# 44 products of ones with ones on TensorE in front of its first turn of q

## The chip, the cores and the metric

One core of one Trainium2 chip. The metric is the device time of one execution in microseconds. It is read from several runs, and one further execution was taken with a profiler. The engines are TensorE (PE; its weight loads are PEld), VectorE (DVE), ScalarE (ACT), GpSimd (POOL) and SyncE (SP), which issues the transfers.

## The reference

Attention with rotary positions for 4 batches of 8 heads, 576 positions and 64 columns a head, followed by a two-layer network on the 2304 rows of 512 columns:

```
q_rot, k_rot = rotate(q), rotate(k)        # x1*cos - x2*sin, x1*sin + x2*cos
scores = q_rot @ k_rot.T / sqrt(64)
attn = exp(scores - max) / (sum + 1e-9)
x = (attn @ v) as [2304, 512]
h = x @ w_in                               # 512 x 2048
out = (h * sigmoid(h)) @ w_out             # 2048 x 512
```

## The kernel before

Heads are worked in pairs p = 0 to 3 of a batch, positions in blocks of 128. Batch 0 is special. Its q and k are rotated in fp32 and turned (transposed) on TensorE, while those of the later batches are split into two f16 parts and turned by transfers. The products of the network run on TensorE in f16 with each operand split into two parts. Once the first weights are ready, they are woven between the scores of the later batches.

The work is a list of named steps in a `Plan`. A table of numbers and letters, `ORDER`, written out by hand, says in which order they are issued and on which engine (t TensorE, d VectorE, a ScalarE, p GpSimd, s SyncE's queue). Each engine runs its own instructions strictly in that order. A step waits for the steps whose results it reads and for a buffer that it reuses.

At the start, for pair 0, k and q are loaded, and VectorE multiplies each by the sine table into a buffer `rt` (L515, and L517 for the last block) and by the cosine table into a buffer `n`. TensorE then turns both into one place and adds them there (`qP`, L529 to L539): 12 products with the identity matrix, which lie in PSUM afterwards and are copied out to `Tq` and `Tk` (`qE`, L551 on ScalarE, L340 on VectorE). The tag `rt` has two buffers and the tag `n` two. The turn of q writes a tile of the pool `s3`, the turn of k one of the pool `s`. For pair 1, VectorE rotates q and GpSimd rotates k, by the same lines.

Beside this the weights of the network come in blocks of 256 hidden columns. For each block, ScalarE and GpSimd bring the 64-bit numbers into fp32 (L839, L844, L846), VectorE joins their parts (L852, called the weight step below), TensorE sums their squares (`trace`, L365, called the trace products), VectorE and TensorE work out a scale from that, and the weights are split. The scores of batch 0 are L1000, their row maxima L1005, the exponentials L1008, and the turned exponentials L1013.

The order on TensorE at the start is: turn of q for pair 0, turn of k for pair 0, trace products of the first block of w_out, the first pair of scores.

The kernel also holds 84 steps `wk` ("keep"), each of two products of a tile of ones. All of them stand in `ORDER` with the letter z, and a step with z issues nothing. The ones are set by one memset (L1391), number 0 of the plan, which VectorE runs after the rotations of pair 0. They are also read by other products (L591, L701, L769, L895).

Of the kernel before, what the change touches and what calls it, by code (L numbers as in the profile page):

```python
# [21 lines left out]
N_KEEP = 84  # L22
# [22 lines left out]
572a 125d 580s 582a 573d 134s 135t 136d 115p 581a 766t 583d 767d 754t 755a 116t 768a 140s 145s 127t 128a 117d 150s
576s 131d 151t 118s 152d 769t 584s 130p 575d 146d 132t 142d 578a 771t 141p 770a 91s 119t 120d 577a 147p 772d 161s 585a
586p 756t 773a 757d 163s 156t 157d 158d 758a 774t 759t 775a 587d 159p 590a 105d 579d 591d 143t 133a 107d 588a 589d
592t 760a 121a 137d 139d 593d 153d 602s 594p 595d 776t 598p 144a 777d 596p 162s 778a 781t 782d 1963d 740p 786t 787d
783a 597d 123d 779t 780a 600p 788a 1970d 604a 784t 785a 148t 789t 172d 149d 164a 796t 165a 599p 797d 791t 790a 173d
801t 650s 652a 178p 792d 166t 802d 651a 167d 798a 799t 174p 622s 603a 606s 1964t 601p 179d 1966t 803a 623a 608p 605d  # L50
168d 626s 793a 653d 794t 1965d 1967d 800d 624a 180p 625d 804t 811t 812d 795a 806t 1973t 805a 607a 609d 807d 627a 813a
814t 630t 169p 628a 629d 631d 155d 815a 646s 648p 647a 808a 1977d 170d 632a 612t 633d 642s 610t 611d 809t 634t 613d
810a 635d 614t 636p 649d 615d 616d 160d 816t 817d 821t 826t 644a 643a 818a 822d 823a 819t 820a 637p 827d 828a 617p
645d 620p 621d 654a 1978t 618p 824t 1979a 655d 122s 656t 829t 657d 658t 659d 660d 830a 1971t 831t 847t 1968p 1969p
154s 619d 1972a 1974d 661p 1980t 832d 664p 665d 825a 666a 667p 833a 834a 638a 106s 640a 848d 194s 839t 1984d 1985t
1986a 171d 835d 1987t 1981d 692s 639d 1982d 840d 1983p 741p 836d 181a 1975d 837d 1988d 668s 841a 842d 849a 1976d 693a
182d 850d 843d 851d 1989a 1990p 175a 844a 863t 864d 838s 855t 183s 852a 865a 845d 176p 2075t 866a 856d 857a 871t 209p
641d 2076a 2077d 669a 670a 196a 872d 867d 2082t 853d 177s 858d 873a 672s 887t 868d 854s 2078d 671d 662a 2079d 869d
846s 195a 663d 676a 197t 185s 2083a 2084d 888d 673a 674a 2080t 210p 870s 874a 2085a 675d 203p 889a 2091t 678a 677d
859d 890d 211d 860a 198d 199p 200a 2086d 679d 688s 680t 681d 891d 892a 682p 683a 204d 875d 684a 861d 862s 879t 212p  # L60
880d 881a 893d 903t 2092a 685d 2081t 694a 2093d 876a 205d 696s 877d 695d 698p 686a 882a 883d 206a 184s 895t 884p 207d
896d 690a 2098t 2087t 213d 894s 689a 2089t 691d 897a 898a 899d 904d 697a 1991t 2094a 900p 201d 699d 702t 905a 208s
2095d 885d 703d 700a 701d 687d 704t 705d 906d 2090a 186a 919t 706p 2099a 225s 227a 707p 2100d 920d 710a 921a 907d 712a
901p 1992d 1993d 214s 878s 226a 2088a 711d 2101p 911t 908a 912d 913a 886s 718s 902s 2105t 922d 923d 2102d 228t 708a
229d 2106a 927t 943t 714s 720a 909d 713d 234p 928d 2107d 240d 910s 914a 709d 929a 2096t 930a 924a 2097t 722s 230p 241d
925d 935t 187t 719a 715a 235p 2114t 231a 931d 926s 932a 138s 716a 944d 945a 946a 2108a 936d 721d 188d 933d 947d 937a
236d 934s 242p 717d 959t 237a 960d 2103t 724d 938a 189p 939d 948a 726t 723a 949d 950s 940a 725d 941d 2104t 961a 728a
1994t 915d 727d 729d 730t 243p 244d 942s 731d 2109d 962a 916a 917d 951t 190a 952d 191a 732p 918s 983t 963d 984d 1995a
953a 1996d 733p 734a 735d 2110t 985a 238p 193d 192d 2111d 975t 216s 256s 954a 955d 742p 964a 2115a 232d 967t 976d
# [127 lines left out]
def rope_attention_silu_ffn(  # L197
# [61 lines left out]
    live = {}  # L259

    def buf(tag, *key):
        if (tag, key) not in live:
# [8 lines left out]
            if tag == "s3":  # L271
                live["wk"] = live[tag, key]
# [1197 lines left out]
```

## Time and profile before

| what | value |
|---|---|
| median of 3 runs | 623.91 us |
| the three runs | 620.99, 623.91, 627.9 us |
| the profiled execution, its own time | 619.83 us |
| its span, first to last instruction | 618.0 us |
| TensorE busy in the span | 589.6 us (95%) |
| VectorE, ScalarE, GpSimd busy | 473.0, 404.7, 293.7 us |
| mean granted TensorE clock | 0.988 |

The profiled execution is below all three of the other runs. Sums of instructions are made against its 619.83 us; between the span and this time lie 1.8 us. In the views, us are counted from the first instruction. A row of a timeline gives start, length, engine, line, operation, output and inputs, and in brackets the idle time before it with what ended it. The granted clock (PEclk) is 1.00 for 2.4 GHz and 0.50 for 1.2 GHz.

### The profile page before, as it was taken

Reading aid. Unit: us, or ns where it says so; the run is one execution under the profiler, and the core shown is the slowest. Engines: PE = TensorE matmul, PEld = TensorE weight load, DVE = VectorE, ACT = ScalarE, POOL = GpSimd, SP = SyncE. Lnnn points to the kernel's source line nnn. Section 1 sums busy time; section 2 is a strip of 40 time slices with the busy share of each in tenths; the row PEclk is TensorE's granted clock in tenths of the full one; section 3 lists DMA queues with packets and bytes.
Section 4 is the critical chain, followed back from the end, with each engine's and each line's share of the span. In section 5 each row is a group of like instructions: output and inputs, shape, how many; then the busy total and the mean of one; then the engine's idle time right before and its main releaser. Section 6 shows DMA issues by size and latency. Waiting matters only on the chain.

```text
span 618.0 us, 12474 instructions
## 1 busy us (share of the span) xinstructions
PE 589.6 (95%) x4484; PEld 391.1 (63%) x4484; DVE 473.0 (77%) x1046; ACT 404.7 (65%) x846; POOL 293.7 (48%) x306
## 2 busy tenths in 40 slices
PE   1999998999999999999999999999999999999997
PEld 1766755555666666666666666666666666666663
DVE  2788889999898899999888898897888674322312
ACT  3477989998888777777757786677664653322321
POOL 0647665375744676443755356452556662010131
PEclk9977999999999999999999999999999999999999
DMA  7968149997979999998956899887966656100201
GB/s 227 301 223 295 34 111 213 246 224 158 158 154 207 148 166 171 169 192 176 187 101 152 152 201 169 191 147 131 156 110 112 116 101 95 34 2 2 52 1 34
DMA packets 208910, 89.92 MB, mean 146 GB/s; under 512 B 187984, under 2 KB 192592, under 8 KB 208848
## 3 DMA queue, kind: packets, MB, share of 16 engines
q1 hardware_dynamic: 208688, 88.84, 68.8%
q8 instruction: 35, 0.57, 0.4%
q10 hardware_dynamic: 160, 0.30, 0.3%
q14 instruction: 27, 0.22, 0.1%
HBM read 35.49 MB, written 4.72 MB: 65 GB/s over the span
## 4 chain that ended last, share of the span: by engine, by line
PE 74%; DVE 8%; ACT 7%; DMA 5%; issue 3%; SPq 1%; POOL 1%; ACTq 0%; POOLq 0%; DVEq 0%
PE m L1342 27%; PE m L1285 26%; PE s L1128 7%; PE pv L1230 7%; DMA pt<-pn 2%; PE s L1000 2%; ACT e L1162 1%; PE s L1134 1%; DMA w_in<-in_k_dram 1%; DMA vh<-vh 1%; DMA w_out<-in_q_dram 1%; ACT pn L346 1%; DVE small L1149 1%; DVE pn L352 1%; PE s L1013 1%
## 5 line engine op out<-in xcount | busy, mean ns | idle before, releaser
L1285 PEld LDWEIGHTS <-w_in 128*128 128x128 f16 x1728 | 166.6, 98 | 33.0 <-issue 5.0
L1285 PE MATMUL m<-xh,w_in 128*128 128x256 f16 x1024 | 178.2, 273 | 1.8 <-DVE g L1301 1.8
L1342 PE MATMUL m<-w_out,gh 128*128 128x512 f16 x576 | 171.6, 379 | 0.0
L1285 PE MATMUL m<-xl,w_in 128*128 128x256 f16 x512 | 139.5, 273 | 0.0
L1162 ACT ACTIVATE e<-s,small 128x576 f32<-128x576 f32 x128 | 98.8, 772 | 41.4 <-DVE s L1144 19.7
L1342 PE MATMUL m<-w_out,gl 128*128 128x512 f16 x288 | 109.1, 379 | 0.0
L1301 DVE SCALAR_TENSOR_TENSOR g<-g,m 128x512 f32<-128x512 f32 x72 | 49.1, 682 | 60.5 <-ACT g L1297 31.8
L352 DVE SCALAR_TENSOR_TENSOR pn<-e,small,pn 128x576 f16<-128x576 f32 x93 | 83.3, 899 | 6.9 <-ACT pn L346 4.1
L1342 PEld LDWEIGHTS <-gh 128*128 128x128 f16 x576 | 52.0, 99 | 54.5 <-issue 3.1
L1297 ACT ACTIVATE g<-m,small 128x512 f32<-128x512 f32 x64 | 43.7, 683 | 54.9 <-PE m L1285 49.8
L346 ACT ACTIVATE pn<-e,small 128x576 f16<-128x576 f32 x75 | 57.4, 770 | 16.8 <-DVE small L1176 12.9
L1128 PE MATMUL s<-Tk,Tq 128*128 128x512 f16 (+1 forms) x384 | 61.3, 286 | 0.9 <-ACT e L1162 0.6
L1230 PE MATMUL pv<-pt,vh 128*64 128x320 f16 (+1 forms) x504 | 54.1, 290 | 0.0
L340 POOL TENSOR_SCALAR pn<-e,small 128x576 f16<-128x576 f32 x31 | 26.8, 866 | 57.1 <-DVE small L1176 39.2
L1144 DVE TENSOR_SCALAR_CACHE_REDUCE s<-s,small 128x576 f32<-128x576 f32 x59 | 47.9, 817 | 7.2 <-PE s L1128 4.9
L352 DVE SCALAR_TENSOR_TENSOR gl<-g,small,gh 128x512 f16<-128x512 f32 x53 | 43.8, 827 | 11.9 <-ACT gh L346 7.4
L1342 PEld LDWEIGHTS <-gl 128*128 128x128 f16 x288 | 28.2, 98 | 34.0
L355 POOL TENSOR_TENSOR pn<-e,pn 128x576 f16<-128x576 f32 x35 | 45.6, 1302 | 2.9
L1128 PEld LDWEIGHTS <-Tq 128*128 128x128 f16 x384 | 28.9, 99 | 27.2 <-issue 4.5
L1151 DVE TENSOR_REDUCE small<-s 128x1 f32<-128x576 f32 x49 | 36.8, 751 | 9.1 <-PE s L1128 9.0
L340 POOL TENSOR_SCALAR g<-g,small 128x512 f32<-128x512 f32 x19 | 16.4, 863 | 56.1 <-ACT gh L346 37.6
L340 POOL TENSOR_SCALAR e<-e,small 128x576 f32<-128x576 f32 x35 | 28.6, 817 | 29.2 <-ACT pn L346 23.1
(213 smaller groups left out, 1034.0 us busy)
## 6 DMA issues: line engine op xcount, KB each, us to landing
w_in<-in_moe_w_in_dram SPq DMA_DIRECT2D x4, 1024.0 KB, 6.9
w_out<-in_moe_w_out_dram SPq DMA_DIRECT2D x4, 1024.0 KB, 8.9
out_dram<-ob SPq DMA_DIRECT2D x28, 128.0 KB, 2.4
io<-in_q_dram SPq DMA_DIRECT2D x12, 288.0 KB, 3.2
io<-in_k_dram SPq DMA_DIRECT2D x12, 288.0 KB, 3.6
io<-in_v_dram SPq DMA_DIRECT2D x12, 288.0 KB, 4.0
Tk<-Tk SPq DMA_DIRECT2D x22, 144.0 KB, 3.0
ring<-in_moe_w_in_dram SPq DMA_DIRECT2D x3, 1024.0 KB, 7.9
```

The costliest lines, as they stand in the source:

```text
L340: e.tensor_scalar(out=out, in0=in0, scalar1=s1, scalar2=s2, op0=ALU.mult, op1=ALU.bypass if s2 is None else ALU.mult)
L346: act.activation(hi, src, AF.Copy, scale=s)
L352: dve.scalar_tensor_tensor(out=lo, in0=src, scalar=s, in1=hi, op0=ALU.mult, op1=ALU.subtract)
L355: e.tensor_tensor(out=lo, in0=src, in1=hi, op=ALU.subtract)
L1128: pe.matmul(o, tq[:, j, 2 * c:2 * c + 2, :], kt[:, r0:r1, js], start=(n == 0), stop=(n == 1))
L1144: dve.tensor_scalar(out=t, in0=t, scalar1=cc[1], scalar2=None, op0=ALU.mult, op1=ALU.min, accum_out=m_of(1, 2),)
L1162: act.activation(buf("e", i), buf("s", i)[:, 0:S], AF.Exp, bias=m_of(1, 2), scale=-1.0 if fused[i] else cc[0], accum_out=m_of(2, 3),)
L1230: pe.matmul(o[64 * j:64 * j + 64, 0:m], vt[part][:, j, s, :], pt[:, a, j, 0:m], start=(z == 0), stop=(z == len(steps) - 1),)
L1285: pe.matmul(t[:, c, 0:n], w[:, wz, kk, fs], xx[:, kk, 0:n], start=(kk == 0 and x == 0), stop=(kk == KD - 1 and x == 2),)
L1297: act.activation(g[:, :, 0:n], t[:, :, 0:n], AF.Tanh, scale=th_v[units[u][0]][:, i:i + 1])
L1301: dve.scalar_tensor_tensor(out=g, in0=g, scalar=1.0, in1=t, op0=ALU.add, op1=ALU.mult)
L1342: pe.matmul(o, gs[gz][:, c, ts], w[:, wz, c], start=(first and c == 0 and x == 0), stop=(last and c == 1 and x == 2),)
```

## The change

The 84 steps that issue nothing are taken out of the plan, and with them their numbers in `ORDER` (all later numbers become 83 smaller). In their place comes one step `keep` on TensorE: 44 products of the ones (as bf16, 128 by 128) with the ones read four times over (512 columns), each written over the one before in a tile of the pool `s3` that nothing reads. The step stands in `ORDER` second, right behind the memset of the ones, which comes first. The turn of q for pair 0 depends on it. Apart from the two entries and the renumbering the table is the same.

```
-N_KEEP = 84
+N_KEEP = 44
...
-556s 92s 89s 97s 88s 85s 93d 98d 558a 557a 87s 559d 86s 99d 100t 564a 565d 560s 561a 562p 94d 95t 108s 113s 102s 90s
-101a 0d 1z 2z 3z 4z 5z 6z 7z 8z 9z 10z 11z 12z 13z 14z 15z 16z 17z 18z 19z 20z 21z 22z 23z 24z 25z 26z 27z 28z 29z 30z
...
+0d 1t 473s 9s 6s 14s 5s 2s 10d 15d 475a 474a 4s 476d 3s 16d 17t 481a 482d 477s 478a 479p 11d 12t 25s 30s 19s 7s 18a
...
-            if tag == "s3":
-                live["wk"] = live[tag, key]
...
-            n = add("qP", key + (nm,), "t", tr, [n, y, ("ident",)], [nb, rt, sb], it)
+            n = add("qP", key + (nm,), "t", tr, [n, y, ("ident",)] + ([] if p else [("keep",)]), [nb, rt, sb], it)
...
-        w_1 += [("sc2", "w", 1)] + keep if (u, i) == (0, 0) else []
+        w_1 += [("sc2", "w", 1)] if (u, i) == (0, 0) else []
...
-    def add_keep(z):
-        def f(e):
-            if e == "t":
-                if "wk" not in live:
-                    buf("s3", "wk")
-                o = live["wk"][:, 640:1024].rearrange("p (a n) -> p a n", a=3)
-                for _ in range(2):
-                    pe.matmul(o, ones_b, ones_b[:, None, :].to_broadcast([128, 3, 128]), start=True, stop=True)
-
-        return add("wk", (z,), "zt", f, [("ones",)])
-
-    keep = [add_keep(z) for z in range(N_KEEP)]
+    def keep():
+        o = buf("s3", "keep")[:, 0:512].rearrange("p (a n) -> p a n", a=4)
+        for _ in range(N_KEEP):
+            pe.matmul(o, ones_b, ones_b[:, None, :].to_broadcast([128, 4, 128]), start=True, stop=True)
+
+    pl.add(("keep",), "t", keep, [("ones",)], [bk("s3", "keep")])
```

TensorE at the start of the program, before: the branch into the program, then the turn of q for pair 0. `s3` is the tile it writes, `id_t` the identity, `n` and `rt` the two rotated halves.

```order
L1466 UNCONDITIONAL_BRANCH [waits barrier_Pool_Activation_PE_DVE_SP_release]
L529 MATMUL s3_166<-id_t_125,n_162 128x128 [waits DMAHW2_49,DVE_49]
L529 MATMUL s3_166<-id_t_125,rt_151 128x128
...
L534 MATMUL s3_166<-id_t_125,n_162 128x64 [waits DVE_49]
L534 MATMUL s3_166<-id_t_125,rt_151 128x64
...
L529 MATMUL s_187<-id_t_125,n_183 128x128 [waits DVE_49]
```

And now:

```order
L1454 UNCONDITIONAL_BRANCH [waits barrier_Pool_Activation_PE_DVE_SP_release]
L1391 LDWEIGHTS ones_126 [waits DVE_49]
L1391 MATMUL s3_137<-ones_126 128x512
...
L523 MATMUL s3_212<-id_t_125,n_208 128x128 [waits DMAHW2_49,DVE_49,PE_49]
L523 MATMUL s3_212<-id_t_125,rt_197 128x128
...
L528 MATMUL s3_212<-id_t_125,n_208 128x64 [waits DVE_49]
```

In front of the turn stand 44 pairs of a weight load and a product, of which one is shown; the first waits for VectorE's memset, and the turn of q stands behind the last of them.

VectorE around the memset, before: the end of the rotations of pair 0 (`n_183` is k's), the memset, the rotation of q for pair 1 and the weight step of w_out.

```order
L515 TENSOR_TENSOR n_183<-w_in_119,cos_t_123 128x4x64 x2
L517 TENSOR_TENSOR n_183<-ob_138,cos_t_123 128x64
L1391 MEMSET ones_126 128x128
L515 TENSOR_TENSOR rt_210<-w_out_120,sin_t_124 128x4x64 [waits DMAHW0_49,DVE_49,PE_49]
L515 TENSOR_TENSOR rt_210<-w_out_120,sin_t_124 128x4x64
L517 TENSOR_TENSOR rt_210<-ob_138,sin_t_124 128x64
L852 SCALAR_TENSOR_TENSOR w_out_120<-w_out_120 128x1024 [waits DMAHW6_49,Activation_49,Pool_49]
```

The start of VectorE's queue now:

```order
L1454 UNCONDITIONAL_BRANCH [waits barrier_Pool_Activation_PE_DVE_SP_release]
L1385 MEMSET ones_126 128x128
L509 TENSOR_TENSOR rt_193<-w_in_119,sin_t_124 128x4x64 [waits DMAHW7_49,DMAHW1_49]
L509 TENSOR_TENSOR rt_193<-w_in_119,sin_t_124 128x4x64
L511 TENSOR_TENSOR rt_193<-ob_184,sin_t_124 128x64 [waits DMAHW2_49,DMAHW3_49,DMAHW1_49,DMAHW0_49]
```

The memset moved from behind the rotations of pair 0 to VectorE's first place. The other engines' rows are the same. Lines behind the table have numbers smaller by 6 in the changed kernel (L509 is L515 of before).

## Rows read from the trace of the kernel before

**Rows 1.** Page, part 4: the chain that ended last, by engine

```profile
PE 74%; DVE 8%; ACT 7%; DMA 5%; issue 3%; SPq 1%; POOL 1%; ACTq 0%; POOLq 0%; DVEq 0%
```

**Rows 2.** The chain in order of time: start us, length us, what

```profile
0.72 0.47 SPq L818
...
11.26 5.60 DMA w_out<-in_q_dram
...
20.18 1.41 PE s L1000 x7
...
44.61 4.94 PE s L1000 x12
...
606.93 6.49 PE m L1342 x30
```

**Rows 3.** Timeline of TensorE, 0 to 60 us

```profile
13.30 0.48 PE L529 MATMUL s<-id_t,n 128*128 128x128 f32 x1 [13.30 <-DVE n L515]
...
18.50 0.42 PE L539 MATMUL s<-id_t,rt 128*64 128x128 f32 x1
19.07 1.11 PE L365 MATMUL mx<-w_out 128*128 128x128 bf16 x8 [0.15 <-DVE w_out L852]
...
22.48 0.27 PE L529 MATMUL s<-id_t,rt 128*128 128x128 f32 x1
...
28.34 0.27 PE L529 MATMUL s<-id_t,n 128*128 128x128 f32 x1
...
29.81 0.39 PE L365 MATMUL pv<-Tk 128*128 128x128 bf16 x4
...
40.45 0.42 PE L529 MATMUL s<-id_t,rt 128*128 128x128 f32 x1
```

**Rows 4.** Busy time by stretch: stretch, length, each engine's busy us (instructions), PEclk, DMA, GB/s

```profile
13.30:19.00 5.70, 5.62 (x24) 4.23 (x24) 3.05 (x9) 2.25 (x5) 1.12 (x1) 1.00 1.12 322
...
40.00:53.50 13.50, 13.44 (x51) 10.06 (x50) 10.14 (x21) 9.36 (x21) 7.15 (x12) 0.50 0.94 360
...
613.40:615.00 1.60, 0.01 (x1) 0.00 (x0) 0.00 (x0) 0.69 (x1) 0.00 (x0) 1.00 0.53 124
...
616.80:618.00 1.20, 0.00 (x0) 0.00 (x0) 0.00 (x0) 0.00 (x0) 0.00 (x0) 0.50 0.00 0
```

**Rows 5.** Timeline of VectorE, 0 to 70 us

```profile
9.74 0.76 DVE L515 TENSOR_TENSOR rt<-w_in,sin_t 128x256 f32<-128x256 f32 x2 [9.74 <-DMA sin_t<-in_sin_dram]
...
14.17 0.17 DVE L1391 MEMSET ones<- 128x128 f32 x1
16.98 0.76 DVE L515 TENSOR_TENSOR rt<-w_out,sin_t 128x256 f32<-128x256 f32 x2 [2.65 <-DMA w_out<-in_q_dram]
...
17.80 1.22 DVE L852 SCALAR_TENSOR_TENSOR w_out<-w_out 128x1024 int32<-128x1024 int32 x1
...
25.62 1.40 DVE L515 TENSOR_TENSOR rt<-w_in,sin_t 128x256 f32<-128x256 f32 x2
...
28.62 1.24 DVE L852 SCALAR_TENSOR_TENSOR ring<-ring 128x512 int32<-128x512 int32 x1
...
38.65 0.69 DVE L852 SCALAR_TENSOR_TENSOR w_in<-w_in 128x512 int32<-128x512 int32 x1
```

**Rows 6.** Timeline of ScalarE, 0 to 30 us

```profile
16.42 0.63 ACT L551 ACTIVATE Tq<-s 128x576 f32<-128x576 f32 x1
```

**Rows 7.** Timeline of GpSimd, 14 to 31 us

```profile
15.43 1.12 POOL L846 TENSOR_SCALAR w_out<-w_out 128x1024 int32<-128x1024 uint16 x1 [15.01 <-DMA w_out<-in_moe_w_out_dram]
19.01 1.43 POOL L515 TENSOR_TENSOR rt<-w_out,sin_t 128x256 f32<-128x256 f32 x2 [2.45 <-DVE w_out L852]
...
25.14 1.61 POOL L515 TENSOR_TENSOR n<-w_out,cos_t 128x256 f32<-128x256 f32 x2
...
28.58 1.86 POOL L515 TENSOR_TENSOR rt<-w_in,sin_t 128x256 f32<-128x256 f32 x2 [1.37 <-PE s L539]
```

**Rows 8.** What TensorE waited for, 20 to 618 us: us in total, times, longest

```profile
PE m L1285 <- DVE g L1301: 1.8, 2, 1.6
```

More of the change, by code (lines that the diff above doesn't have):

```diff
@@ L45 @@
[L45 to L69, printed above, removed]
@@ new lines @@
+2042p 939d 926t 927d 2043t 891s 899s 137p 921d 940d 2046a 2047d 928d 953t 2044t 138a 139a 954d 2048a 140d 182p 156s
+941a 914a 942d 162s 922d 943s 955a 2049d 929a 1917t 1918a 141d 915d 164s 188p 1919d 930d 923a 944t 956a 945D 2056t
+931d 924d 175a 971t 174a 946d 176t 916s 957a 183d 2050t 184p 2057a 972d 177d 958d 925s 947a 2058d 2059a 932d 933d 178p
+179d 962t 163s 2053t 963D 948d 2054d 2060d 2051d 189p 934s 185a 186p 165a 964d 180d 2063t 965a 966a 190d 166t 187s
+2064a 2061t 167d 2065d 168p 191a 967d 2062t 2070t 968a 150d 169d 192d 2066d 973a 969d 195s 2067d 989t 2068t 170a 171d
@@ new lines @@
+974a 2069t 975d 959a 970s 172d 2071a 990D 211s 949d 950a 960d 951d 961s 991a 952s 2072d 992a 2073d 196a 1007t 993d
+1008d 193s 976d 1009d 980t 981d 2074p 977a 978d 194s 1010a 226p 2077t 197t 2078a 998t 198d 982a 204t 994d 979s 2075t
+205d 206t 995a 2079d 2080p 999d 207d 208p 983a 199d 1000a 220d 1052t 1920t 984a 985d 1011a 986a 996d 200a 1001a 209p
+1002a 213a 987d 210d 181d 1053D 988s 2076t 212a 1034t 1003d 1921a 1054a 1035d 2084t 1922d 1012d 221p 2081d 2082t 1004a
+1005d 997s 214t 662d 201a 202d 1055a 1006s 1013d 203d 1025t 215d 1014d 216p 222p 1036a 2085a 1015s 1026D 1037a 2086d
@@ new lines @@
+1038a 1027d 1028a 1039d 1040p 2083t 217d 223a 1043t 1044d 1923t 1029d 1030d 2087a 1031a 1041d 242s 1032d 1016t 1045a
+1042s 1033s 1046a 1047a 2091t 1017d 1018d 1019a 1924d 2088p 1056d 1057d 1925d 1058a 1020a 2092a 1061t 1062D 1063d
+1021d 1022a 1059d 224p 1048d 1070t 1071d 1023d 1064a 1926t 1060s 2093d 2094a 2089t 1079t 1080d 2090t 2098t 1072a 2052s
+1073a 1049p 1050d 1051s 1088t 227p 228d 218d 1081a 1082a 1083a 1084d 1074d 1024s 2095p 1124t 663d 257d 1085a 225s
+1086d 1087s 1125D 229a 230p 1927a 1928d 231s 1126d 2096t 1127a 1065d 1066d 1075d 1076a 2099a 2097t 1089d 1077d 243a
@@ new lines @@
+2100d 1067p 1068d 1128d 1129d 1090a 1069s 1091a 1092a 1106t 1929t 1107D 1108d 2101p 2102d 2105t 1930a 1931d 1133t
+1130p 1109a 2106a 1110d 1078s 1093d 244a 1131p 2107d 1094a 2108p 1132s 2103t 251d 1134D 258p 1111d 219d 273s 245t
+1097t 246d 1135d 1098D 247p 1136a 2104t 1095d 1137d 2109d 248d 1112a 1096s 1113d 2116t 1151t 252d 259d 1114s 2110t
+2113t 1099a 1100a 232s 1101a 1102d 2117a 253d 260p 1103a 2111a 1138d 261p 2118d 1152D 1153a 1154a 1115t 2114a 2123t
+1104d 1116d 1155a 1117a 1139a 2119d 1105s 1142t 262s 1118a 1140p 2120d 1932t 2124a 254a 1119d 1120d 1178t 1141s 2125d
@@ new lines @@
+2121t 1143d 1144d 1121a 1933d 1156d 1122d 1145a 1169t 1146d 1147d 1179D 2122t 2126a 275a 255d 2127d 282p 1180d 2130t
+1123s 1181a 1157a 1182d 1183d 1170d 1171a 288p 256s 1934d 1160t 2131a 2132d 2133a 2128t 1184p 1185p 1148a 233s 2137t
+274a 1161D 2134d 1162d 1149d 1158d 276t 289d 2129t 1163a 277d 2138a 1164a 283d 1172a 278d 1205t 234a 2139d 2140a 1187t
+284p 1206d 1186s 279d 285a 2135t 1173d 263s 1174d 235t 1188D 1207a 1189d 1175d 1176d 2144t 1190a 290p 291a 286d 236d
+292d 237p 238d 1150s 1159s 1208a 1209a 2141d 1177s 264s 1214t 1191a 1192d 1193d 1223t 1210d 249d 250d 1194d 1211a
@@ new lines @@
+1271a 1257d 1259t 315p 1247a 321d 309p 2161a 1298a 2162d 1286t 1258s 1272a 310a 2055s 322a 1248d 1260d 316a 281d 1261d
+1262a 1941t 323d 317d 326s 1263d 1264d 311d 1299d 1300d 1301p 1232t 1942a 1943d 2163t 2164t 2166a 2167d 2168p 1302d
+296a 1287d 1288a 1249s 1303s 2176t 2169d 1233D 1234d 1235a 297t 1265p 1266d 2170t 2173t 324s 2177a 1273d 1274p 1275p
+327a 298d 1277t 328t 299d 300d 301d 2171a 2178d 302d 1289a 303d 1236d 2179a 318s 1237d 2183t 1238p 1267s 1239p 329d
+2180d 1278D 2181t 1322t 1279d 1290a 2184a 335t 2185d 1280a 2174a 1323d 1331t 1324d 1325a 342s 1332d 336d 2190t 1281d
@@ new lines @@
+1282d 330d 1283a 1291d 1284d 337t 351d 2186p 1276s 2187p 1333d 1240s 2191a 338d 325s 2182t 2188t 331p 332p 343a 344a
+345t 1292p 2192d 1285s 1334a 1326a 1327d 1328a 1335d 1313t 1304t 1293p 1305D 1294s 1314D 1315d 346d 347d 1306d 2193a
+2194d 1329d 2197t 1307a 1944t 1336d 1316a 1337p 349d 350d 339p 1330s 1338p 1339s 2198a 352p 334d 1308a 312d 1340t
+1367t 1368D 1369d 348p 2189t 340d 2195t 341d 1945d 2199d 1946d 1370a 1371a 333d 1317a 1372d 1309d 1318d 1319a 1358t
+1359d 1320d 1360d 1361a 2200p 2201d 1310a 357d 1311d 2204t 1341D 1373a 1342a 1343a 1344a 1947t 1403t 1948d 1404D 1949d
@@ new lines @@
+1362a 1363d 1345d 1321s 1374p 2205a 1405a 1346a 1312s 2196t 1375s 2206d 353p 1347d 373s 1348s 2207a 2208d 2202t 2203t
+1406a 1407a 358d 1408d 1409p 1349t 1350D 1351a 1364a 1410d 1365d 354a 355d 2211t 2212a 1352a 1950t 2213d 2214a 2112s
+1411s 1376t 1353d 1354d 1951a 1377d 1378a 388d 1385t 1379a 2215p 2218t 2209t 1386d 1387d 1366s 2219a 2220d 1388a 1394t
+1395D 1355p 1380a 1381d 1389d 1356p 1357s 1390d 1391d 1392d 2210t 1412t 1382a 1393s 2216t 1413D 1396a 1397a 1414d
+1415a 1416a 359d 1439t 356s 360a 382p 1383d 1384s 1440D 2217t 1441d 1417d 1952d 1398d 2221a 1442a 1418a 1419p 1443a
@@ new lines @@
+387s 380d 1456s 2247d 1464d 1465s 365a 1484t 1485D 1486a 2250t 366t 1472a 367d 1496a 363s 2251a 2252d 1487a 368d 406a
+1488a 1473p 2242t 2253d 2254p 1497d 369a 419d 413d 370a 1498d 1475t 1499a 1476D 1500d 2248t 2257t 2258a 1489d 1502t
+2259d 414p 1503d 2249t 1477a 1474s 372d 1490a 1959t 1478a 1479d 2260a 1504d 1505a 1506a 2261d 1520t 1521d 1960a 393s
+371d 1961d 2264t 1491p 381d 1511t 1501s 1522a 1523a 1507d 1508d 2255t 1509d 1512D 1529t 1530D 1513a 2256t 405a 1524a
+1525d 2265a 2266d 407t 408d 409d 1514a 1515a 1531a 1547t 2267a 1480d 1516d 2268d 1526d 1492s 395s 1510s 1527d 2235s
@@ new lines @@
+1517a 415d 2271t 420p 421p 394s 2272a 1548D 1532a 2262t 2263t 2232s 1538t 410p 416p 396a 422a 2273d 2274p 1518d 1539d
+1528s 397t 1481a 1482d 1519s 1540a 1541a 1542a 417d 2278t 1543d 1483s 1556t 2275d 1549a 1550a 2279a 1557d 418s 1551d
+1544p 1545d 1546s 1558d 2269t 411d 423p 398d 399p 2270t 412d 2280d 1559a 1574t 1552d 1553a 1575d 1576a 2276t 1533d
+2281p 1554d 1577a 1583t 1584d 1585d 1534d 1535p 1536d 2282d 435s 1962t 1578a 1579d 1580a 1565t 2285t 1581p 1555s 1586a
+1537s 2277t 400a 444d 1566d 401a 2283t 1567a 1963d 1964d 1560a 1561d 2286a 1568a 450d 1965t 1569a 2287d 1587d 1619t
@@ new lines @@
+462p 1973d 2332a 1672s 2329t 2330t 1695d 1696d 1697d 1698p 1727t 1728D 1729d 463a 1730a 1974t 2333d 1686a 1687d 1688p
+1709t 1710D 1731a 1711a 1718t 1719d 1732d 1720a 1721a 2338t 1699s 1689d 1736t 2334p 1712a 2335d 1733d 1734d 1735s
+1713a 1714d 465d 1690s 2336t 2339a 1715p 1716p 2340d 2341d 1722a 1737D 1975d 1738a 1739a 1740a 2337t 1772t 1773d 1774a
+1775a 2345t 1717s 1723d 464d 2342d 1724p 1725p 1700t 1754t 1741d 1976d 1701D 1742a 1743d 1744s 1702a 1703a 1755d 2346a
+2343t 1704d 1705d 1756d 1757a 1977t 1978d 2344t 1781t 2115s 2347d 1979d 2356t 1745t 1726s 2348d 1782d 1758a 2349p
@@ new lines @@
+1706d 1707d 2357a 2350t 1783d 1759d 1760d 1784a 1785d 2351a 1708s 2358d 1776a 1786d 1746D 1763t 1764d 2353t 1761p
+1747a 2363t 1762s 1748a 2359p 1787d 1788d 2360p 1790t 1791d 2364a 2365d 1792a 1749a 1777d 1750d 2354a 1980t 2370t
+2366a 1981d 1765a 1751p 1752d 1766a 1789s 1778a 1808t 1753s 2367p 2361t 2362t 1767a 1768d 1982d 2371a 1793a 2372d
+1809D 1779p 1780s 1799t 2377t 1810d 1769d 2355s 1770d 1794d 1771s 1800d 1801a 1811a 1795d 1796a 1797d 1798s 1812a
+1813d 1835t 2368t 2369t 2373p 1802a 2374p 1836D 2378a 1803d 1804d 1814a 1815p 1805d 1816s 1826t 1827D 1828d 1837a
@@ new lines @@
+1838a 1853t 2375t 1983t 1829a 1854D 2379d 1806p 1830d 1831d 2380a 1832d 1833p 1984a 1871t 1855a 1856a 2384t 1872D
+1873a 2381d 1857a 1807s 1874a 1858d 1834s 1859d 2385a 1860p 1875d 1876d 1861s 1877a 1817t 1878p 2376t 1879s 1844t
+1818d 1819d 1820a 1821a 2386d 1845d 2387p 2382t 2383t 1846a 1822d 1839a 1823d 1824d 1840d 1862t 1863D 1825s 1864a
+2388d 1841a 2391t 1865a 1866d 1842d 2392a 1843s 1847a 1848d 2393d 2394a 1849d 1985d 2352s 2395d 1867d 2389t 1850a
+1868p 2390t 1869d 2398t 1851p 2399a 2396t 2400d 2397t 2401p 2402d 1986t 2405t 1870s 1987d 1988d 2406a 1852s 2407d
@@ new lines @@
+1989t 1990a 1991d 2403t 2408a 2409d 2416t 2417a 2404t 2410t 2411a 2412s 2418d 2419a 2420d 2423t 2424a 2425d 2413t
+2426p 2414a 2427d 2421t 2430t 2422t 2428t 2431a 2432d 2433a 2437t 2434d 2438a 2439d 2429t 2435t 2444t 2440a 2415s
+2436t 2441p 2445a 2442t 2446d 2451t 2443t 2447a 2448d 2449t 2452a 2453d 2458t 2450t 2454d 2455d 2459a 2460d 2456t
+2461p 2462d 2465t 2466a 2467d 2457t 2463t 2468a 2476t 2469d 2477a 2464t 2478d 2470t 2479a 2480d 2483t 2471d 2473t
+2481t 2484a 2472s 2485d 2486a 2487p 2474d 2490t 2482t 2488t 2491a 2492d 2493d 2497t 2494d 2292s 2489t 2498a 2475s
@@ L166 @@
+2499d 2500p 2501p 2495t 2504t 2505a 2506d 2496t 2502t 2511t 2507a 2508p 2512a 2503t 2509t 2513d 2514p 2518t 2515d
+2519a 2520d 2510t 2516t 2525t 2521d 2522p 2517t 2523t 2526a 2527d 2524t 2528a 2529d 2530t 2533t 2531d 2534a 2532s
+2535s
 """
```

147 lines of the change are left out of this document (48 added, 99 removed).

## Prediction

> **What bounds the kernel now.** I read the chain that ended last first. TensorE holds 74% of it, and most of the rest is work that hands TensorE its operands [rows 1]. So a microsecond lost or won on TensorE early can reach the end, unless another engine has slack for it. The change touches only the start, so I went on to that stretch of the same chain. There TensorE is not the bound: the chain runs through the transfer of q for pair 1 (issued at 11.26, 5.60 us), VectorE's rotation and weight step on those data, then TensorE's trace products and the first pair of scores, which end at 21.59 [rows 2].
>
> Then TensorE's timeline [rows 3]. Its first turn of q starts at 13.30, and the turns of q and k end at 18.50 + 0.42 = 18.92. One product of a turn takes 0.42 us here, 0.27 us at 22.48, and 0.42 us again at 40.45. The stretches show 0.50 for 40.0 to 53.5, the lower level (1.2 GHz), and 1.00 for 13.3 to 19.0 [rows 4]. I believe the durations, not the 1.00: products as long as those at 40.45 ran at the lower level, and the column shows no change before its first recorded one. So TensorE starts at 1.2 GHz and is at 2.4 GHz by 22.48. That is what warm-up products can change: what stands between 13.30 and about 20 us.
>
> **The change, step by step.** (a) The memset of the ones goes from 14.17 on VectorE to its first place. It takes 0.17 us, and VectorE waits until 9.74 for its first data [rows 5]; at its old place 2.65 us of waiting for a transfer follow it. Cost and gain: nothing. The 84 old entries issued nothing in the kernel before, and their removal costs nothing either.
>
> (b) The 44 products. They can start when the memset is done; the first work of the program, SyncE's first transfer, starts at 0.72 [rows 2], so I put their start at 1.0 (an estimate). Thirty products with 512 columns took 6.49 us at the upper level [rows 2], 0.216 each. All at the upper level: 9.5 us, done at 10.5. All at the lower, at twice the time: 19.0 us, done at 20.0. Before, TensorE went from 0.42 to 0.27 us a product somewhere between 18.92 and 22.48, so after some 6 to 9 us of products. With 6 us at the lower level, 14 products are done by 7.0, and 30 more take 6.5: done at 13.5. That is the start of the turn of q within 0.2 us. ScalarE copies that turn out only at 16.42, behind another instruction [rows 6], so this delay is free.
>
> (c) The two turns at the upper level. Twelve products took 29.81 - 28.34 = 1.47 us there [rows 3], so both turns take 2.9 and end at 16.4, 2.5 us earlier than 18.92. Nobody on the chain waits for them: TensorE's next work, the trace products at 19.07, waits for VectorE's weight step of 17.80, and that for the transfer. So the 2.5 us turn into idle time. What is won on the chain is that these trace products, 1.11 us long [rows 3], run at up to twice the pace: at most 0.5 us.
>
> (d) What the earlier turn sets free. GpSimd's first rotation starts at 19.01 and is put down to VectorE's weight step [rows 7]. That step ends at 17.80 + 1.22 = 19.02, too late to be the cause; the turn of k ends at 18.92. The tiles say the same: the rotated halves have two buffers, taken by k, q, then q of pair 1 (VectorE, already at 16.98 while k was still being turned, so in q's old place) and then k of pair 1 (GpSimd, in k's old place). So GpSimd waited for the turn of k. It will be let go at 16.4, is free at 15.43 + 1.12 = 16.55, and its data were issued ahead of those that VectorE gets at 16.9. It starts 2.1 to 2.4 us earlier, on top of VectorE's rotation and weight step from 16.98 to 19.02, which it did not touch before.
>
> Beside such a GpSimd rotation VectorE slows down: the same two rotation products took 0.76 us alone at 16.98 and 1.40 at 25.62 beside GpSimd's of 25.14; a weight step of 512 took 0.69 at 38.65 and 1.24 at 28.62 beside GpSimd's of 28.58 [rows 5, 7]. So the rotation costs 0.6 more, and the weight step of 1024, at 1.24/0.69 = 1.8 times 1.22, 1.0 more: 1.6 in all. GpSimd's four products take twice 1.43 and two short ones, over 3 us even alone, so they cover the whole stretch. Bounds: 0 (GpSimd is let go by something else) and +1.6. I take +1.5, by the weight step's own row. The chain's trace products then start at 20.6 in place of 19.07.
>
> The Trainium skill (SBUF — State Buffer, "SBUF: two separate sides") says that VectorE instructions with two SBUF inputs and GpSimd share one pair of ports, which one holds for a whole instruction while the other is blocked. This trace shows less: 0.75 and 1.43 us of lone work took 1.88 us together, from 25.14 to 27.02, so they overlapped in part. By the rule VectorE's stretch would lose more than the rows give.
>
> (e) TensorE's idle time from 16.4 to 20.6. After the start the longest wait in front of a TensorE group is 1.6 us [rows 8], and the clock stayed up through it. At the end, the last products finish at 613.4; 1.00 is still shown until 615, and 0.50 from 616.8 on [rows 4]. So idleness brings the clock down within 3.4 us, and 4.2 us are coming. I expect the lower level again for the trace products and the first scores. The scores took 1.41 us [rows 2]; at half the clock 2.8, so +1.4 if all of them run low. If the clock stays up, -0.5 as in (c). If it stays low for 6 us of work, as after 13.30, TensorE loses 3.0. I take +0.9, since part of the scores may still run high.
>
> Sum: 0 + 0 + 1.5 + 0.9 = +2.4 us at about 24 us. VectorE and TensorE are near full until the end, so I let all of it through. The profiled execution took 619.8 (a span of 618.0 and 1.8 around it), so it would become 622.2. The median of the runs stands at 623.9, 4.1 above it; with the same addition the forecast is 626.3. Its own bounds are -0.5 and +1.6 + 3.0 = +4.6: 623.4 to 628.5.
>
> **Rivals.** 1. A clean gain: GpSimd is let go by something else or its overlap is harmless, and the clock stays up. For it: the releasing row does name VectorE, and a wait of 1.6 us did no harm. Against: the ends of the two instructions. It gives -0.5: 623.4.
>
> 2. The later low stretch shrinks. From 40.0 to 53.5 TensorE runs at 0.50 and is busy 13.44 us [rows 4]; the scores of 44.61 alone hold the chain for 4.94 us [rows 2]. Should the new timing carry the clock across, up to 6.7 us of TensorE time come back; ScalarE and VectorE also hold the chain there, so some 4 reach the end: 620. Against: the work before 40 is the same and in the same order.
>
> 3. The other side: the gap after the turns costs a long low stretch. After the clock fell before 40, it stayed low for over 13 us although TensorE was busy. The same from 20.6 on costs 13.5/2 = 6.7 us of TensorE time, of which 0.5 was lost before too, and with (d) +7.7 at most. It decides if TensorE stands still beyond what the clock tolerates: 631.6.
>
> The Trainium skill (TensorE: Matmul & The Clock Gate, "Part 4: PE-mode transpose") says that transposing products do not engage the upper level as others do. Here the 24 of the turns up to 29.81 ran at 0.27 us, which does not agree; by the rule rival 3 would be likelier.
>
> 4. The products do not do what they are for: the clock does not rise with them. Then they end at 20.0 and the turn of q comes 6.7 us late: 630.6. Against: the clock did rise in the first 9 us of products before.
>
> **How the numbers follow.** The forecast (turns early, idle time, a slower first weight step) gets 0.50, rival 1 0.24, rival 2 0.09, rival 3 0.10, rival 4 0.07. The predicted time is 626.3. The range, 620.0 to 631.0, reaches from rival 2 nearly to rival 3, and the three runs before are themselves 7 us apart. One per cent is 6.2 us, about what a measurement of this kernel can tell from no change: faster than 617.7 needs rival 2 with all of its 6.7 us (0.04); slower than 630.1 is rivals 3 and 4 with little else (0.15); the rest, 0.81, is no change that can be told.
>
> **What would show it.** Right, step by step: products of the turns of 0.27 us from about 13.4; their end near 16.4; GpSimd's first rotation before 17; VectorE's rotation at about 1.4 us and its weight step over 2; the trace products after 20; a 0.50 between 17 and 25. Wrong: a weight step that still ends at 19.0 would fell (d); 1.00 and products of 0.27 us throughout up to 30 would fell (e); a time below 620 would mean that the stretch after 40, not the start, was decided by the change.

## The result and the profile after

The changed kernel takes 625.86 us (median of 20 runs, 623.79 to 632.24), the kernel before, in 20 runs beside it, 623.22 (618.78 to 627.9). The ratio is 1.0066, with a 95% interval of 1.0042 to 1.0091: the change costs 0.4 to 0.9%, less than the one per cent set as the border and clear of zero. The two medians differ by 0.42%, at the lower end of that interval. The forecast was 626.3, which is 0.4% above the 623.91 that it started from. Runs more than 1.5% above the fastest run of their kernel are left out of every ratio: one run of e4, one of the kernel before beside e5 and one beside e6 and e7.

The profiled execution of the changed kernel took 624.24 us, with a span of 622.5. First TensorE's timeline from 0 to 60 us, where [rows 3] answers:

```profile
1.04 11.80 PE L1391 MATMUL s<-ones 128*128 128x512 bf16 x44 [1.04 <-DVE ones L1385]
13.62 0.30 PE L523 MATMUL s<-id_t,n 128*128 128x128 f32 x1 [0.79 <-PE s L1391]
13.75 0.27 PE L523 MATMUL s<-id_t,rt 128*128 128x128 f32 x1
...
20.94 1.11 PE L359 MATMUL mx<-w_out 128*128 128x128 bf16 x8 [4.18 <-DVE w_out L846]
21.98 2.88 PE L994 MATMUL s<-Tk,Tq 64*128 64x64 f32 x10
...
26.36 0.42 PE L523 MATMUL s<-id_t,rt 128*128 128x128 f32 x1
```

The products of ones do what they are for: they end at 12.84, and the turns run at 0.27 us a product. Then TensorE idles for 4.18 us in front of the trace products, the first scores take 2.88 us in place of 1.57, and the next turn, at 26.36, is back at 0.42. The idle note of the turn of q names TensorE's own products, but they ended 0.8 us earlier; VectorE's cosine product for q, below, ends at about 13.5 and is what came last. (In e4, where TensorE's own products end far earlier, the row names VectorE.)

VectorE, 0 to 45 us, beside [rows 5]; L999 is the row maxima:

```profile
0.81 0.17 DVE L1385 MEMSET ones<- 128x128 f32 x1 [0.81 <-PEq L1433]
...
12.76 0.76 DVE L509 TENSOR_TENSOR n<-w_in,cos_t 128x256 f32<-128x256 f32 x2
...
17.42 1.52 DVE L509 TENSOR_TENSOR rt<-w_out,sin_t 128x256 f32<-128x256 f32 x2 [2.96 <-DMA w_out<-in_q_dram]
...
19.12 1.76 DVE L846 SCALAR_TENSOR_TENSOR w_out<-w_out 128x1024 int32<-128x1024 int32 x1
...
24.73 1.42 DVE L999 TENSOR_REDUCE small<-s 128x1 f32<-128x576 f32 x2 [2.35 <-PE s L994]
...
33.42 0.75 DVE L999 TENSOR_REDUCE small<-s 128x1 f32<-128x576 f32 x1
```

The last of these rows is the maximum of the second pair of scores. In the kernel before it is:

```profile
29.78 0.74 DVE L1005 TENSOR_REDUCE small<-s 128x1 f32<-128x576 f32 x1
```

GpSimd, beside [rows 7]:

```profile
15.88 1.11 POOL L840 TENSOR_SCALAR w_out<-w_out 128x1024 int32<-128x1024 uint16 x1 [15.46 <-DMA w_out<-in_moe_w_out_dram]
17.07 1.59 POOL L509 TENSOR_TENSOR rt<-w_out,sin_t 128x256 f32<-128x256 f32 x2
...
19.08 2.39 POOL L509 TENSOR_TENSOR n<-w_out,cos_t 128x256 f32<-128x256 f32 x2
```

GpSimd starts its rotation at 17.07 in place of 19.01, without idling in front of it. It now stands beside VectorE's rotation (1.52 in place of 0.76) and weight step (1.76 in place of 1.22). Before, both were over when GpSimd began.

The chain from 15 to 35 us shows what this is worth (start, length, what), beside [rows 2]:

```profile
11.71 5.59 DMA w_out<-in_q_dram
...
19.20 1.70 DVE w_out L846
...
20.94 1.11 PE mx L359 x8
22.05 2.81 PE s L994 x8
```

From VectorE's start to the trace products it is 20.94 - 17.42 = 3.52 us, against 19.07 - 16.98 = 2.09 before: +1.43. The scores on the chain take 2.81 against 1.41, but these are eight products here and seven before; the whole group of ten, by TensorE's timelines, takes 2.88 against 1.57: +1.31. The 0.44 us by which VectorE starts later here belong to the transfer.

The granted clock by stretch, beside [rows 4]:

```profile
1.04:5.30 4.26, 4.26 (x11) 1.50 (x12) 0.00 (x0) 0.96 (x1) 0.00 (x0) 1.00 0.78 228
5.40:12.80 7.40, 7.40 (x35) 3.16 (x33) 2.79 (x8) 2.16 (x2) 0.00 (x0) 1.00 0.73 173
...
16.60:19.00 2.40, 0.16 (x2) 0.00 (x0) 1.58 (x3) 1.43 (x3) 2.32 (x4) 1.00 1.19 291
19.10:29.20 10.10, 8.26 (x41) 6.78 (x42) 4.88 (x14) 3.57 (x7) 4.53 (x7) 0.50 0.89 314
...
43.00:46.30 3.30, 3.30 (x17) 2.76 (x15) 3.20 (x7) 3.03 (x9) 0.22 (x1) 0.50 0.96 310
```

Eleven products of ones touch the first 4.26 us and 35 the next 7.4. So the first ten or so ran at half the pace of the others, although the column shows 1.00 for both: as in the kernel before, it says nothing ahead of its first recorded change. From 19.1 to 29.2 it shows 0.50: the clock fell while TensorE idled, and stayed low through the trace products, the first scores and the next turn.

### The profile page after: what moved, and what is told of

Read it like the earlier page. It is cut to its first block, busy times and chain, and to the rows that moved or that the text cites. A ratio compares the mean times of both kernels' runs of the same rounds, so it can differ in the third digit from the quotient of the medians.

```text
span 622.5 us, 12562 instructions
## 1 busy us (share of the span) xinstructions
PE 599.7 (96%) x4528; PEld 394.6 (63%) x4528; DVE 473.0 (76%) x1046; ACT 404.4 (65%) x846; POOL 295.2 (47%) x306
## 4 chain that ended last, share of the span: by engine, by line
PE 72%; DVE 10%; ACT 7%; DMA 4%; issue 3%; POOL 2%; SPq 2%; POOLq 0%; DVEq 0%; ACTq 0%
PE m L1336 26%; PE m L1279 25%; PE s L1122 7%; PE pv L1224 7%; PE s L994 1%; PE s L1128 1%; ACT e L1156 1%; DMA w_in<-in_k_dram 1%; DMA pt<-pn 1%; DMA w_out<-in_q_dram 1%; ACT pn L340 1%; DVE small L1143 1%; DVE pn L346 1%; DVE gl L346 1%; DMA Tk<-Tk 1%
## 5 line engine op out<-in xcount | busy, mean ns | idle before, releaser
L346 DVE SCALAR_TENSOR_TENSOR pn<-e,small,pn 128x576 f16<-128x576 f32 x93 | 81.9, 884 | 7.9 <-ACT pn L340 5.0
```

The lines of the kernel that those rows point to most:

```text
L346: dve.scalar_tensor_tensor(out=lo, in0=src, scalar=s, in1=hi, op0=ALU.mult, op1=ALU.subtract)
```

## The experiments

The theory (A): two costs add up. The early end of the turn of k lets GpSimd's rotation onto VectorE's, which makes the weight step and the trace products late; and the idle time so made brings TensorE's clock down. Rival B: the clock alone costs. Rival C: the cost lies elsewhere, in the products themselves or later in the kernel. Each ratio is to the kernel before on the same chip, in runs beside it. The first four ran together, beside 35 runs of the kernel before (median 621.74).

**e1: GpSimd's rotation held behind the weight step.** `held` is a tile of one column that nothing else reads; the instruction waits for VectorE's weight step.

```
 def r0(e, ...):
+    if e == "p" and p == 1 and nm == "k":
+        times(pool, held, raws[0, "out", 0][0]().bitcast(F32)[:, 1:2], 1.0, 1.0)
     product(e, 1, x4()[:, :, ::-1, :], x8()[:, ::-1, :], sin_t, turned)
```

> The changed kernel, with one GpSimd instruction of one column in front of its rotation of k for pair 1, which reads a column of VectorE's weight step of w_out, so that this rotation starts behind the weight step as it did before. Theory A (two costs: GpSimd's early rotation slows VectorE, and the idle time brings TensorE's clock down): VectorE's rotation takes 0.76 us again and the weight step 1.22; the trace products start at 19.0 to 19.6 in place of 20.9; TensorE idles about 3 us in front of them, so its clock may still fall; time 1 to 3 us under the changed kernel. Rival B (the clock alone costs): the trace products come earlier, but the time stays within 1 us of the changed kernel. Rival C (the cost is not in this stretch at all): as B, and e2 and e3 as slow as well.

Measured: 623.27 us (12 runs), ratio 1.0035 (1.0007 to 1.0062). Its TensorE:

```profile
18.98 1.10 PE L360 MATMUL mx<-w_out 128*128 128x128 bf16 x8 [2.40 <-DVE w_out L849]
20.01 2.25 PE L997 MATMUL s<-Tk,Tq 64*128 64x64 f32 x10
```

and its VectorE:

```profile
16.89 0.76 DVE L510 TENSOR_TENSOR rt<-w_out,sin_t 128x256 f32<-128x256 f32 x2 [2.62 <-DMA w_out<-in_q_dram]
17.70 1.22 DVE L849 SCALAR_TENSOR_TENSOR w_out<-w_out 128x1024 int32<-128x1024 int32 x1
...
31.16 0.75 DVE L1002 TENSOR_REDUCE small<-s 128x1 f32<-128x576 f32 x1
```

and its clock:

```profile
19.00:20.60 1.60, 1.60 (x14) 1.37 (x16) 0.30 (x2) 0.00 (x0) 1.59 (x4) 1.00 1.09 393
20.80:27.50 6.70, 6.70 (x34) 5.42 (x31) 3.42 (x10) 3.90 (x7) 4.49 (x8) 0.50 1.03 349
```

VectorE's two steps are back at 0.76 and 1.22 to the hundredth, and the trace products at 18.98. GpSimd's rotation starts behind them:

```profile
19.16 1.42 POOL L510 TENSOR_TENSOR rt<-w_out,sin_t 128x256 f32<-128x256 f32 x2
```

So it was GpSimd that slowed them. An idle time of 2.40 us is left, and the clock still falls, at 20.6 to 20.8, while TensorE is busy again. By the ratios about half of the loss is left, but the interval of e1 overlaps that of the change.

**e2: TensorE kept busy behind the turn of k.**

```
 def tr(...):
...
+    if p == 0 and nm == "k":
+        ones_b = ones.bitcast(BF16)[:, 0:128]
+        o = buf("pv", "keep2")[:, 0:512].rearrange("p (a n) -> p a n", a=4)
+        for _ in range(20):
+            pe.matmul(o, ones_b, ones_b[:, None, :].to_broadcast([128, 4, 128]), start=True, stop=True)
```

> The changed kernel, with 20 more products of ones with ones on TensorE behind the turn of k for pair 0, in a tile of the pool pv, to keep TensorE busy until the trace products. Theory A: the clock stays up over the trace products and the first scores, which take 0.55 and 1.4 us in place of 1.1 and 2.8; the trace products still start at about 20.9; the first maxima start at about 23.0 (24.73 in the changed kernel, 21.61 before); time 1 to 3 us under the changed kernel and 1 to 2 us over the kernel before. Rival B: as fast as the kernel before. Rival C: as slow as the changed kernel.

Measured: 623.2 us (12 runs), ratio 1.002 (0.9993 to 1.0048).

```profile
16.51 4.48 PE L540 MATMUL pv<-ones 128*128 128x512 bf16 x20
20.83 1.11 PE L359 MATMUL mx<-w_out 128*128 128x128 bf16 x8
21.86 1.57 PE L999 MATMUL s<-Tk,Tq 64*128 64x64 f32 x10
```

VectorE's rotation and its maximum of the second pair of scores:

```profile
16.97 1.67 DVE L509 TENSOR_TENSOR rt<-w_out,sin_t 128x256 f32<-128x256 f32 x2 [2.93 <-DMA w_out<-in_q_dram]
...
31.53 0.74 DVE L1004 TENSOR_REDUCE small<-s 128x1 f32<-128x576 f32 x1
```

The first maxima start at 23.36, and the stretch from 6.7 up to 40.6 shows 1.00:

```profile
6.70:20.80 14.10, 14.04 (x76) 7.35 (x74) 8.07 (x17) 5.42 (x7) 5.18 (x6) 1.00 0.90 265
20.80:24.00 3.20, 3.20 (x26) 2.56 (x25) 0.94 (x3) 0.00 (x0) 0.67 (x2) 1.00 1.08 361
24.00:40.60 16.60, 14.95 (x111) 11.06 (x109) 16.50 (x39) 10.22 (x18) 10.29 (x16) 1.00 0.46 152
```

The late trace products stay, the slow scores go. One surprise is in these rows: the trace products take 1.11 us here at 1.00, and 1.11 us in the changed kernel at 0.50. They do not follow the clock, so my gain of up to 0.5 us on them does not exist.

**e3: both, with 13 products behind the turn of k in place of 20.**

> The changed kernel with both: GpSimd's rotation held behind VectorE's weight step, and 13 more products behind the turn of k. Theory A: trace products at 19.0 to 19.6 at the upper level, first maxima at about 21.2, 0.4 us earlier than in the kernel before; time 0 to 1 us under the kernel before. Rival B: the same as e2. Rival C (the 44 products cost by themselves, wherever the clock is): 2 to 4 us over the kernel before, as the changed kernel.

Measured: 620.29 us (12 runs), ratio 0.9991 (0.9957 to 1.0025).

```profile
16.37 2.97 PE L543 MATMUL pv<-ones 128*128 128x512 bf16 x13
19.17 1.10 PE L360 MATMUL mx<-w_out 128*128 128x128 bf16 x8
20.20 1.57 PE L1002 MATMUL s<-Tk,Tq 64*128 64x64 f32 x10
```

With both costs taken away the loss is gone, with the 44 products still in front. That ends rival C. The first maxima start at 21.70, against 21.61 before and 21.2 expected: TensorE at the upper level from the first turn on gives nothing here, since the stretch waits for a transfer. The trace products start 0.3 us behind the weight step (it ends at 18.85), when the 13 products are nearly through, so these probably cost a little themselves. The profiled run, 625.13 us, is one of the longer ones of e3, with the lower level at 39 to 42 and 46 to 52 us.

**e4: 16 products in front in place of 44** (`N_KEEP = 16`).

> The changed kernel with 16 products in front in place of 44. They end at 6 to 8 us, TensorE then idles until 13.6, and the clock is down again when the turn of q starts. Theory A: the turns take 5.6 us as in the kernel before, the turn of k ends at about 19.2, GpSimd's rotation starts there, VectorE's weight step takes 1.22; time within 1 us of the kernel before. Rival C: 2 to 4 us over it.

Measured: 623.34 us (12 runs), ratio 1.0013 (0.9978 to 1.0047). The products end at 6.74, the clock falls again, and the turns run low:

```profile
12.20:18.80 6.60, 5.28 (x24) 4.23 (x24) 3.86 (x11) 2.91 (x4) 1.15 (x1) 0.50 1.07 336
```

Here the recorded 0.50 stands over the turns, and GpSimd's rotation starts at 19.16, VectorE's steps take 0.76 and 1.22, the trace products start at 19.18. No difference to the kernel before can be told. It is the faster turn, not the products, that sets the loss off.

**e5: GpSimd let go early in the kernel before**, without any product of ones, by another buffer for its rotated half. It ran beside 15 other runs of the kernel before (median 620.0).

```
 def turned(which, nm=nm):
     if which:
+        if p == 1 and nm == "k":
+            return buf("e", "rt")
         return buf("rt", 0, p, nm).rearrange("p r u d -> p (r u d)")
```

> The kernel before, without any product of ones, but with the rotated half of k for pair 1 in a buffer of the tag e, so that GpSimd need not wait for the turn of k. Theory A: GpSimd's rotation starts at about 16.6, VectorE's rotation takes about 1.5 us and its weight step about 1.8, the trace products start at about 20.8 in place of 19.07 while the turns still run at the lower level and end at 18.9; time 1 to 3 us over the kernel before. Rival B (the clock alone costs): the trace products are late, but the time is within 1 us of the kernel before.

Measured: 625.45 us (10 runs), ratio 1.0078 (1.005 to 1.0107), so a loss as large as the change's and larger than the 1 to 3 us that were expected. GpSimd:

```profile
16.70 1.59 POOL L517 TENSOR_TENSOR e<-w_out,sin_t 128x256 f32<-128x256 f32 x2
```

VectorE:

```profile
17.04 1.53 DVE L517 TENSOR_TENSOR rt<-w_out,sin_t 128x256 f32<-128x256 f32 x2 [2.64 <-DMA w_out<-in_q_dram]
...
18.75 1.76 DVE L854 SCALAR_TENSOR_TENSOR w_out<-w_out 128x1024 int32<-128x1024 int32 x1
```

TensorE and its clock:

```profile
16.74 0.42 PE L531 MATMUL s<-id_t,rt 128*128 128x128 f32 x1
...
17.28 0.27 PE L531 MATMUL s<-id_t,n 128*128 128x128 f32 x1
...
20.57 1.12 PE L365 MATMUL mx<-w_out 128*128 128x128 bf16 x8 [2.30 <-DVE w_out L854]
21.62 2.88 PE L1002 MATMUL s<-Tk,Tq 64*128 64x64 f32 x10
```
```profile
17.30:20.50 3.20, 0.97 (x8) 0.47 (x6) 3.20 (x4) 0.65 (x1) 3.20 (x5) 1.00 1.15 327
20.70:37.60 16.90, 16.90 (x76) 13.51 (x76) 9.05 (x24) 5.32 (x10) 4.96 (x9) 0.50 0.54 184
```

This shows that GpSimd waited for the turn of k and not for the weight step that the row named, and that its early start alone makes both costs. In this execution the clock had risen at about 17, within the turn of k; TensorE then idled 2.30 us, and 17 us at the lower level followed. So the two costs are not independent: a late weight step can make the idle time, as the early turns do in e1, and the clock falls behind it. Rival B falls as far as it calls GpSimd harmless. The profiled run, 627.05 us, is longer than the median of e5; it had a second stretch at the lower level, 16.8 us from 44.6 on.

**before2 and after2: each kernel profiled once more.**

> The kernel before once more, one look. The runs of it lie 9 us apart. If the later stretches at the lower clock make this spread, they will lie elsewhere or be of other lengths than 39.9 to 53.6, and the span will differ by about half of the difference of their lengths; if not, the granted clock will be the same and the span will differ all the same. The start (turns at the lower level, trace products at 19.1) should be as before.

> The changed kernel once more, one look. Theory A: the start as in its first profile (turns at the upper level, trace products near 20.9 and the clock down around them), the later stretches at the lower level at other places or of other lengths.

The kernel before took 618.33 us, with trace products at 19.21 and one low stretch near 40 that is far shorter than the 13.5 us of [rows 4], and another near 122 that the first profile did not have:

```profile
39.80:43.10 3.30, 3.30 (x17) 2.57 (x15) 3.30 (x8) 3.30 (x8) 0.00 (x0) 0.50 0.89 274
...
121.70:124.90 3.20, 3.20 (x14) 1.75 (x13) 3.17 (x11) 3.20 (x9) 3.12 (x4) 0.50 1.09 218
```

The changed kernel took 624.05 us, with VectorE's steps at 1.53 and 1.76, the trace products at 20.58 behind 3.96 us of idle time, and 0.50 from 19.7 to 29.8. Up to the trace products each kernel's start repeats itself to 0.4 us, and these are the transfer's; the later low stretches do not repeat. In the 35 runs beside e1 to e4 the time of the kernel before goes with its mean granted clock: the six with 0.992 or more took 617.77 to 620.26 us, the six with 0.983 or less 623.86 to 626.28.

**e6: the low stretch near 40 attacked in the kernel before. e7: the same on top of e3.** Four products of ones among the one-column products at 37 to 39 us.

```
 def mm_first():
     o = ps()
+    feed(3)
...
+    feed(1)
```

> The kernel before, with four products of ones with ones (512 columns, read by nobody) at 37 to 39 us: three in front of the one-column products of the first v scale and one behind them. Each profile so far shows the lower level from about 39 to 44 on, for 3.4 to 17 us. If the thin one-column work there brings the clock down and the low stretch costs what its length says, the clock stays up over 40, the turn of q near 40 runs at 0.27 us a product, and the time falls by 1 to 4 us. If the clock falls all the same, or the work behind waits for VectorE and ScalarE anyway, the time is within 1 us of the kernel before, or up to 0.5 us over it for the four products.

> The changed kernel with GpSimd's rotation held, the 13 products behind the turn of k, and the four products at 37 to 39 us. If both stretches matter and add up: as e6, and up to 1 us better. If the warm start gives nothing by itself (as e3 against the kernel before): the same as e6.

Measured, beside 23 runs of the kernel before (median 621.06): e6 621.21 us, ratio 1.0009 (0.998 to 1.0037); e7 621.98 us, ratio 1.0002 (0.9973 to 1.003). In e6's profile the turn of q near 40 ran at 0.27 us a product, as hoped, and the clock fell afterwards:

```profile
40.66 0.27 PE L529 MATMUL s<-id_t,rt 128*128 128x128 f32 x1
...
43.48 1.29 PE L903 MATMUL mx<-small,ones 128*128 128x1 f32 x6 [1.29 <-ACT ring L888]
```

TensorE, being faster, waits 1.29 us for ScalarE, and the low level comes behind that wait, for some 10 us in these two stretches:

```profile
39.00:50.00 11.00, 9.61 (x45) 6.86 (x45) 7.95 (x21) 7.85 (x18) 4.96 (x11) 0.71 0.99 359
50.00:60.00 10.00, 9.47 (x56) 7.42 (x56) 8.83 (x15) 8.65 (x17) 6.25 (x6) 0.80 0.92 320
```

It looks like the course of the change, a faster TensorE that idles in front of a late operand. That the wait brought the clock down is not shown: in the kernel before the clock falls at 39.9 although TensorE had no idle time over 0.32 us from 32 us on. No version was found that beats the kernel before.

## Why the prediction was right

(a) Right: the memset stands at 0.81, and its old place was waiting time.

(b) Right, and a little too long: 13.5 was forecast for the end of the 44 products, it was 12.84 (13.44 in e2, 12.00 in e1), before the turn of q could start in any case. The lower level lasted for 4.3 us of products and not for 6.

(c) Right that the turns end near 16.4 (16.76) and that nobody on the chain waits for them. Wrong in its only gain: the trace products take 1.11 us at either level (e2 against the changed kernel). What they follow instead is not tested; their weight loads take 0.116 us each at 1.00 (e2) and 0.125 at 0.50 (changed kernel), and eight of these make most of it.

(d) Right in mechanism, and in size as a whole: +1.5 was taken, +1.43 measured in the first profile. Its parts missed in opposite directions, so the fit of the sum is partly luck: +0.76 on the rotation where 0.6 had been said, +0.54 on the weight step where it was 1.0, and small parts. The weight step took 1.76, not over 2, and GpSimd began at 17.07, just behind its own step before, not ahead of 17. Why the weight step of 1024 suffered less than the ratio of the 512 one had it is not shown; the second pair of GpSimd's products, which stood beside it, got long too (2.39 in place of 1.41). e1 undoes the slowdown, e5 makes it alone.

(e) Right in mechanism, too small: the first scores ran low as a whole (+1.31) and the clock stayed low until 29.2, so that VectorE waited another 1.50 us for the next turn. Net, +0.9 had been taken. By the row maximum of the next scores (29.78 before, 33.42 after) the kernel is 3.6 us late, of which 0.44 belong to the transfer: 3.2 against the +2.4 of the sum.

The end: 626.3 lies only 0.4 us from the median measured, and that is partly luck too. The start lost more than the sum had, and the three runs that the forecast began from had a median 0.7 us above that of the twenty. The ratio of 1.0066 of some 623 us is +4.1 us, the medians differ by 2.6, and the interval reaches from 2.6 to 5.7. As far as this tells, what was lost by 33 us was not won back, as the prediction had let it through. The reason it gave holds for TensorE alone, which is busy for 95% of the span; VectorE, with 77%, is not near full until the end. How much of a single run's time lies in the start cannot be read from its total, because the later low stretches differ from run to run: the two first profiles differ by 4.4 us in time, although the kernel before had 13.5 us of low level after 40 and the changed one two stretches of 3.3 to 3.4 us, from 43 and from 67.

Rival 1 is excluded by e1 and e5, rival 4 by the turns at 0.27 us. Rival 2 cannot be told from the differences between runs: after 40 us the kernel before had 13.5 us at the lower level in one profile and two stretches of some 3.3 in the other, the changed kernel two of some 3.3 in both. Nor does e6 show what a clean passage over 40 would give, since there the low level only came later, behind the wait for ScalarE, and no time came back. Rival 3 was the nearest to the course of things after the forecast, though not in its time: 10 us at the lower level in the changed kernel, 17 in e5.

Of the two rules of the Trainium skill, SBUF — State Buffer, "SBUF: two separate sides", has VectorE and GpSimd exclude each other for whole instructions. The trace agrees on which engines slow each other, less on how much: the two rotations, 0.76 and 1.43 us alone, took 1.87 together here (17.07 to 18.94), so they overlapped in part again. That transposes do not engage the upper level (TensorE: Matmul & The Clock Gate, "Part 4: PE-mode transpose") was not seen. The 24 products from 13.62 on all ran at the pace of the upper level, which the products of ones had brought; and in e5 the clock rose at about 17.2, when TensorE had run nothing but turning products since 13.37.

The totals leave the shares of the two costs open: e1 (+0.35%) and e2 (+0.20%) together make about what the change costs, but the interval of e2 reaches zero. The traces tell them for the start. From VectorE's rotation to the row maximum of the second scores it is 29.78 - 16.98 = 12.80 us before and 33.42 - 17.42 = 16.00 in the changed kernel: +3.20 (+3.53 between the second profiles of the two). In e1, where the clock's part is left, it is 31.16 - 16.89 = 14.27 (+1.47). In e2, where the slower steps are left, it is 31.53 - 16.97 = 14.56 (+1.76), of which some 0.2 go to the added products, which the trace products wait for. In e3 it is 13.06 (+0.26). So at that point the two costs are of about the same size and add up. What of each reaches the end stays open, and so does why the clock falls near 40.

## What to carry to other kernels

Before warming TensorE up for a stretch, look at what its first late operand waits for. Here that was a transfer, so the faster TensorE only idled in front of it, and the clock fell again in the idle time or just behind it. Look also for who waits behind the work that gets faster, a buffer handed to GpSimd above all: an instruction that starts earlier can land on a neighbour that the chain goes through. Doubt a row that names a releaser whose end comes after the start it is said to release; here the buffers in their order of use named another, and a run with another buffer (e5) bore them out.

## What the runs showed of the hardware that was not expected

The eight trace products with 128 columns and a weight load each took 1.10 to 1.12 us at either level of the clock, while the products of the turns went from 0.42 to 0.27.

Idle times of 2.3 to 4.2 us in front of the trace products were followed by the lower level in both profiles of the changed kernel, in e1 and in e5, and the fall could come after TensorE was busy again (e1: idle until 18.98, down between 20.6 and 20.8). Where the gap was filled (e2, e3) it did not fall there. Near 40 us it fell without such a gap: in the kernel before, the longest idle time from 32 to 39.9 us is 0.32.

The level rose while nothing but fp32 transposes ran: in e5 the products of the turn went from 0.42 us at 16.74 to 0.27 at 17.28, without any other product before them.

The same program had one low stretch of 13.5 us after 40 in one execution and two of some 3.3 in another. Over many runs the mean granted clock goes with the time, which spreads over 9 us for one kernel.
